# Linear attention with a feed-forward layer behind it: loads of v on other queues and in other memory, q transposed to contiguous columns, work of the first batches on other engines, and a new written order

## The chip, the cores and the metric

The kernel runs on one core of a Trainium2 chip. A core has five engines with instruction queues of their own: TensorE (PE, matmuls; its weight loads are shown as PEld), VectorE (DVE), ScalarE (ACT), GpSimd (POOL) and SyncE (SP). Each runs its instructions in the order in which they are written and waits on semaphores for the others. DMAs are issued from SP's queue and from GpSimd's, and are carried by 16 DMA engines. The metric is device time in microseconds (us). The kernel before takes 392.82 us, the median of 3 runs (391.64 to 393.09).

## The reference

Eight batches, eight heads, 576 tokens of 64 values. Each row of q and k is projected to 128 features, the largest absolute feature of the row is subtracted, and both signs go through the exponential. Then linear attention, and on its output, 4608 tokens of 512 values, a gated layer of width 1536:

```python
def phi(x):
    proj = np.einsum('bhsd,df->bhsf', x, w_phi)
    proj = proj - np.max(np.abs(proj), axis=-1, keepdims=True)
    return np.concatenate([np.exp(proj), np.exp(-proj)], axis=-1)
q_p, k_p = (phi(q), phi(k))
kv = np.einsum('bhsf,bhsd->bhfd', k_p, v)
z = np.sum(k_p, axis=2)
num = np.einsum('bhsf,bhfd->bhsd', q_p, kv)
den = np.einsum('bhsf,bhf->bhs', q_p, z)[..., None] + 1e-06
...
gate = np.maximum(x @ w_gate, 0.0)
val = x @ w_val
out = gate * val @ w_out
```

## The kernel before, in words

Each batch has 512 tokens, handled as four chunks of 128, and a remainder of 64; the remainders of two batches form a pair (four pairs, which make a ninth group for the feed-forward layer). The kernel is a list of small steps, named `do_xx` in the code. One long string, ORDER, names every step with its arguments (batch, group of heads, chunk, sign) and, after a colon, the PSUM banks that it uses. A loop walks the string and issues each step, so ORDER fixes by hand the order of each engine's queue, of SP's and of GpSimd's DMA issues too. Heads go in three groups, 0 to 1, 2 to 4 and 5 to 7.

The steps that matter here:

- Loads. `lk`, `lq`, `lm`, `ln` fetch k, q and their remainders on GpSimd's queue, converting to bf16. `lv` fetches v in fp32 on SP's queue into the one tile `vn`, and `lw` its remainder into `vm`. For batch 0, v lies without the column of ones. `wl` and `wo` fetch the weights of the feed-forward layer on GpSimd's queue, in thirds; `wp` and `wq` fetch the projection's weights on SP's, and `wc` and `wd` convert them on VectorE. `gt` is a tiny DMA that holds SP's queue until a group of k has landed. `ms` are memsets.
- k. For batch 0, `k0`, `k1`, `k2` transpose k on PE, copy it (VectorE) and project it. For later batches `kt` and `ku` transpose k in 32x32 blocks on VectorE, scattering the columns, and `kr` projects it on PE. `kx` takes the largest absolute value on VectorE, `ke` the exponentials of both signs on ScalarE, `kk` the factors exp(-m) and exp(m) into `ek`.
- v. `vs` and `vr` multiply v by these factors on GpSimd; `vo` writes the factors as the column behind v, which gives the denominator. `kv` multiplies k's features and v on PE, `kd` copies the result to the tile `kv` on VectorE.
- q. `qt` transposes q in 32x32 blocks on VectorE into `qT` (L607 to L614). `qc` (or `qs`, one quarter of it) projects it on PE: `q_cols` (L616) issues two sets of four matmuls, 32 rows and 512 columns each. `qe` takes the exponentials, `qx` the maxima by column, `qy`, `qz`, `qu`, `qw` turn the maxima into a factor a token.
- Output of attention. `nu` multiplies q's features with `kv` on PE; `nt`, `nv`, `nr` combine the two signs and take the reciprocal on VectorE. Then `ny` normalizes on VectorE or `nx` on GpSimd, into `xu`. For batch 0, `xp` transposes `xu` on PE and `xc` copies it into the tile of x^T; later `xt` does both as a DMA transposition on SP's queue. The four tiles of x^T are used in turn, batch by batch.
- Remainders: `mt`, `mc`, `me`, `mx`, `my`, `mz`, `mu`, `mw`, `mn`.
- Feed-forward: `fv` and `fg` (a group of 128 of the 1536 columns, four matmuls of 512 tokens each), `va` copies the value part on ScalarE, `ga` takes relu and product on VectorE; `fo` multiplies by the output weights in three parts, `oc` copies, `od` stores. For batch 0, two thirds of the columns are done by token chunk as `pv`, `pg`, `pa`, `pb`, so that they can begin when the first chunk of x^T is there. `zz` are dummy matmuls.

Of the kernel before, what the change touches and what calls it, by code (L numbers as in the profile page):

```python
# [8 lines left out]
FP32 = mybir.dt.float32  # L9
BF16 = mybir.dt.bfloat16  # L10
# [6 lines left out]
ms.0 wp ms.5 wq lk.0.0 ms.4 lk.0.1 lm.0.1 ms.3 lm.0.0 lk.0.2 wc id zz.10:0 k0.1:0 gt.0 lv.0.0 ms.2  # L17
lw.0.0 wd k1.1:0 lq.0.0 k0.0:1 k1.0:1 wl.0.1 zz.1:2 k2.1:2345 ke.0.1.3.1:5 ke.0.1.2.1:4 if
kx.0.1.0:2 k2.0:6701 kx.0.0.2:0 kx.0.0.1:7 kx.0.0.3:1 ke.0.1.3.0:5 lw.0.1 lq.0.1 ke.0.0.0.0:6
ke.0.0.0.1:6 ke.0.1.1.1:3 kx.0.0.0:6 kx.0.1.2:4 kx.0.1.3:5 k0.2:6 kk.0.0.0 ke.0.1.0.0:2  # L20
ke.0.1.0.1:2 kk.0.0.1 ke.0.0.2.1:0 kx.0.1.1:3 k1.2:6 wl.1.1 wl.0.0 lv.0.1 ke.0.0.1.1:7 wl.1.0
lm.1.1 ke.0.0.1.0:7 ke.0.1.1.0:3 qt.0.0.0 ke.0.0.3.1:1 qt.0.1.0 k2.2:5267 ke.0.1.2.0:4 kx.0.2.1:2
vr.0.0.0 kk.0.1.0 ke.0.0.2.0:0 qs.0.0.1:3 qx.0.0.1:3 vr.0.1.0 kk.0.1.1 ke.0.2.0.0:5 vs.0.0.1
ke.0.2.2.1:6 qs.0.0.0:4 ke.0.2.1.1:2 qx.0.0.0:4 qs.0.1.0:0 ke.0.2.1.0:2 kx.0.2.3:7 ke.0.0.3.0:1
qe.0.0.0.0:4 qx.0.1.0:0 kx.0.2.0:5 ke.0.2.3.0:7 kx.0.2.2:6 qy.0.0:2 qz.0.0:2 qe.0.1.0.0:0 vr.0.0.1
kk.0.2.0 vr.0.1.1 vs.0.0.0 qt.0.0.1 qs.0.1.1:1 ke.0.2.0.1:5 vo.0 ke.0.2.2.0:6 qx.0.1.1:1 kv.0.0:2
kd.0.0:2 qe.0.0.1.1:3 qt.0.1.1 qs.0.0.2:5 qx.0.0.2:5 vo.1 kk.0.2.1 qe.0.1.0.1:0 ke.0.2.3.1:7
qe.0.0.0.1:4 vs.0.1.0 vs.0.1.1 kv.0.1:6 kd.0.1:6 qs.0.1.3:2 qx.0.1.3:2 qe.0.0.1.0:3 lv.0.2
vs.0.2.0 vs.0.2.1 vo.2 qs.0.1.2:0 qe.0.1.2.1:0 qu.0.0 qw.0.0 nu.0.0.0:7 qe.0.1.3.1:2 qy.0.1:4
qz.0.1:4 ms.1 qu.0.1 qw.0.1 nt.0.0.0:7 nu.0.0.1:6 kv.0.2:3 nt.0.0.1:6 nv.0.0.0:7 qe.0.1.1.1:1  # L30
kd.0.2:3 qs.0.0.3:4 zz.1:7 nu.0.0.2:7 ln.0.0 lq.1.2 qx.0.0.3:4 zz.1:3 qy.0.3:3 nt.0.0.2:7
nv.0.0.1:6 qe.0.1.1.0:1 nu.0.1.1:1 qe.0.1.3.0:2 qe.0.0.2.0:5 nv.0.0.2:7 nr.0.0 lk.1.3 nu.0.1.0:2
nt.0.1.0:2 ny.0.0 nu.0.1.2:6 qe.0.1.2.0:0 qx.0.1.2:0 qz.0.3:3 zz.6:7 xp.0.0:7 xc.0.0:7 lm.1.0
nt.0.1.2:6 qe.0.0.3.1:4 nv.0.1.0:2 qy.0.2:0 qz.0.2:0 qe.0.0.3.0:4 nt.0.1.1:1 qe.0.0.2.1:5 qu.0.2
qw.0.2 nu.0.2.1:4 nu.0.2.0:5 nu.0.2.2:3 wl.1.2 nv.0.1.2:6 pv.0.0:7 pa.0.0:7 nv.0.1.1:1 ln.0.1
qu.0.3 nt.0.2.0:5 nr.0.1 nt.0.2.1:4 qw.0.3 wl.0.2 nu.0.3.2:2 nu.0.3.0:0 ny.0.1 nv.0.2.1:4
nt.0.2.2:3 nt.0.3.0:0 pg.1.0:6 nv.0.2.2:3 pv.1.0:1 xp.0.1:7 xc.0.1:7 nv.0.2.0:5 nv.0.3.0:0
pg.0.0:4 nr.0.2 ny.0.2 nt.0.3.2:2 pb.0.0:4 nv.0.3.2:2 qt.1.0 nu.0.3.1:3 nt.0.3.1:3 pv.1.1:7
pv.0.1:5 xp.0.2:0 pa.0.1:5 pa.1.0:1 xc.0.2:0 nv.0.3.1:3 pg.0.1:4 pb.0.1:4 pa.1.1:7 pg.1.1:2
qc.1.0:5103 qe.1.0.2.0:0 qe.1.0.3.0:3 qe.1.0.0.1:5 qe.1.0.2.1:0 pv.0.2:4 pa.0.2:4 nr.0.3 ny.0.3  # L40
# [36 lines left out]
qx.2.1.0:7 ln.1.1 fv.1.4:1 kv.2.1:0 qx.2.1.2:2 kk.2.2.1 lw.3.0 kv.2.0:3 kt.3.1 qy.2.0:5 qz.2.0:5
qe.2.1.3.0:4 kd.2.0:3 kk.2.2.0 kt.3.2 nr.8.0 qe.2.1.0.1:7 kd.2.1:0 fv.1.9:6 qe.2.1.0.0:7 fg.1.5:2
qu.2.0 va.1.4:1 qw.2.0 ga.1.5:2 nu.2.0.0:5 va.1.9:6 vs.2.2.0 vs.2.2.1 ln.1.0 ku.3 qe.2.1.3.1:4
qt.3.1 fv.1.3:7 nu.2.1.0:3 nt.2.1.0:3 kt.3.0 fv.1.6:1 va.1.3:7 nu.2.1.1:0 lv.3.1 nt.2.0.0:5  # L80
nv.2.0.0:5 nt.2.1.1:0 nv.2.1.1:0 kv.2.2:2 kd.2.2:2 fg.1.6:6 lv.3.3 qt.3.0 kr.3.0:4750 va.1.6:1
ga.1.6:6 ke.3.0.0.0:4 ke.3.0.1.1:7 lq.4.2 ke.3.0.0.1:4 nu.2.0.2:1 fg.1.3:2 nv.2.1.0:3 nu.2.0.1:6
nt.2.0.2:1 nv.2.0.2:1 nx.8.0 kx.3.0.0:4 xt.8.0 ga.1.3:2 ke.3.0.2.1:5 kx.3.0.2:5 fv.1.7:3 od.0.2
od.0.3 fg.1.4:1 nu.2.2.0:4 ga.1.4:1 nt.2.0.1:6 va.1.7:3 nv.2.0.1:6 ke.3.0.3.0:0 fv.1.10:2
nu.2.2.2:3 ke.3.0.1.0:7 nt.2.2.2:3 fv.1.8:1 kx.3.0.1:7 va.1.10:2 nv.2.2.2:3 fg.1.7:6 ke.3.0.3.1:0
ke.3.0.2.0:5 va.1.8:1 lm.4.1 kr.3.1:2753 ke.3.1.0.0:2 ke.3.1.1.0:7 lk.4.3 kx.3.0.3:0 kk.3.0.1
vr.3.1.1 ke.3.1.1.1:7 nu.2.2.1:0 ke.3.1.2.1:5 vr.3.0.1 nu.2.1.2:1 nt.2.2.0:4 nv.2.2.0:4 ga.1.7:6
ke.3.1.3.1:3 nt.2.2.1:0 fo.1.1.0:4 lv.3.2 nv.2.2.1:0 ke.3.1.3.0:3 kx.3.1.0:2 fv.1.11:6
ke.3.1.2.0:5 fg.1.10:0 lm.4.0 va.1.11:6 nt.2.1.2:1 nv.2.1.2:1 fg.1.9:1 kx.3.1.3:3 nr.2.0
# [146 lines left out]
def kernel(  # L236
# [16 lines left out]
    P = 128  # L253
# [70 lines left out]
    def xT(g):  # L324
        return xT_mix if g == B else xT_of(g)
# [620 lines left out]
```

## Time and profile before

| | |
|---|---|
| median of 3 runs | 392.82 us (391.64 to 393.09) |
| the profiled execution | 392.23 us, its span 390.4 us |
| PE busy | 370.0 us (95%) |
| VectorE busy | 281.3 us (72%) |
| ScalarE busy | 234.0 us (60%) |
| GpSimd busy | 157.1 us (40%) |
| PE's share of the chain that ended last | 84% |
| VectorE's share of it | 7% |

The span is what the profiler saw of the program; the execution's time is 1.8 us longer. Busy is the time in which an engine had an instruction in work. For PE the ends of matmuls are modelled and matmuls overlap, so small gaps between them count as busy. The chain that ended last goes back from the last instruction, at each step to what released it or to the one before it on its engine. A line of a group reads: line of the code, engine, operation, output and input tiles, shapes, count, then busy us, mean ns of one, and idle time before it.

### The profile page before, as it was taken

What the parts mean: (1) busy time and instruction counts of PE and PEld (TensorE: products, weight loads), DVE (VectorE), ACT (ScalarE), POOL (GpSimd) and SP (SyncE); (2) the same over time, 40 slices, a digit from 0 to 9 for tenths busy, and PEclk for the clock granted to TensorE, in tenths of its full rate; (3) what the DMA queues carried; (4) which work ended last, traced back from release to release, by engine and by line L of the source; (5) the groups of instructions that cost most, each with busy time, mean ns of one, the idle gap of its engine ahead of it and who ended that gap; (6) DMA issues with size and microseconds to landing.
All of it is one profiled execution on the core that took longest, in us unless ns stands there. A gap on an engine that the chain in (4) does not pass through costs nothing.

```text
span 390.4 us, 9052 instructions
## 1 busy us (share of the span) xinstructions
PE 370.0 (95%) x3536; PEld 196.8 (50%) x3536; DVE 281.3 (72%) x661; ACT 234.0 (60%) x560; POOL 157.1 (40%) x173
## 2 busy tenths in 40 slices
PE   3579999979999999999999999999999999999995
PEld 2247964645554465445544655465446544444442
DVE  3978998999999768489996978699856833320330
ACT  1855489898488822498779445988694313422312
POOL 8396048278544912258156622561561130100000
PEclk9999999989999999999999999999999999999999
DMA  8989995559497590272951695113620022101104
GB/s 109 212 158 189 198 185 95 110 90 135 67 194 105 100 168 13 70 140 52 179 99 56 89 206 84 38 38 66 143 81 3 2 54 109 40 0 55 54 0 107
DMA packets 91135, 38.01 MB, mean 97 GB/s; under 512 B 64214, under 2 KB 86486, under 8 KB 91094
## 3 DMA queue, kind: packets, MB, share of 16 engines
q0 software_dynamic: 33600, 14.18, 29.0%
q1 hardware_dynamic: 57494, 23.28, 26.5%
q8 instruction: 27, 0.44, 0.5%
q14 instruction: 14, 0.11, 0.1%
HBM read 37.95 MB, written 9.44 MB: 121 GB/s over the span
## 4 chain that ended last, share of the span: by engine, by line
PE 84%; DVE 7%; ACT 3%; POOL 2%; DMA 2%; issue 1%; DVEq 0%; ACTq 0%; POOLq 0%
PE bank L831 43%; PE bank L886 23%; PE bank L583 5%; PE bank L683 4%; PE bank L620 2%; PE bank L468 2%; ACT kp L515 2%; DMA kn<-in_k_dram 2%; POOL vs L544 1%; DVE kT L452 1%; DVE qT L611 1%; PE bank L857 1%; DVE h L875 1%; DVE mk L523 1%; DVE t L704 1%
## 5 line engine op out<-in xcount | busy, mean ns | idle before, releaser
L849 DVE SCALAR_TENSOR_TENSOR h<-bank,val 128x512 bf16<-128x512 f32 x100 | 66.6, 680 | 52.1 <-PE bank L831 27.6
L886 PE MATMUL bank<-wo,h 128*128 128x512 bf16 x432 | 100.2, 379 | 0.0
L846 ACT CAST val<-bank 128x512 bf16<-128x512 f32 x100 | 58.3, 607 | 62.1 <-PE bank L831 42.4
L515 ACT ACTIVATE kp<-bank 128x384 bf16<-128x384 f32 x192 | 81.9, 524 | 20.0 <-PE bank L468 8.8
L831 PE MATMUL bank<-xT,wv 128*128 128x512 bf16 x352 | 87.2, 382 | 0.0
L831 PE MATMUL bank<-xT,wg 128*128 128x512 bf16 x352 | 86.7, 379 | 0.3 <-DVE mk L523 0.3
L726 POOL TENSOR_TENSOR xu<-u,r 128x512 bf16<-128x512 f32 x32 | 33.1, 1042 | 104.9 <-DVE r L722 99.0
L635 ACT ACTIVATE qp<-bank 128x512 bf16<-128x512 f32 x128 | 70.1, 626 | 8.3 <-PE bank L620 6.6
L544 POOL TENSOR_TENSOR vs<-vn,ek 128x780 bf16<-128x780 f32 (+3 forms) x48 | 64.0, 1344 | 17.8 <-ACT ek L532 14.7
L886 PEld LDWEIGHTS <-h 128*128 128x128 bf16 x432 | 40.5, 98 | 46.9 <-issue 1.8
L831 PEld LDWEIGHTS <-wv 128*128 128x128 bf16 x400 | 37.1, 98 | 42.6 <-issue 3.9
L831 PEld LDWEIGHTS <-wg 128*128 128x128 bf16 x400 | 37.2, 98 | 41.9 <-issue 1.5
L523 DVE TENSOR_REDUCE mk<-bank 128x3 f32<-128x384 f32 x96 | 49.7, 545 | 7.6 <-ACT ob L895 4.7
L643 DVE TRANSPOSE_TENSOR_REDUCE maxq<-bank 128x16 f32<-128x512 f32 x64 | 42.7, 693 | 6.1 <-PE bank L620 3.0
L895 ACT COPY ob<-bank 128x512 f32<-128x512 f32 x36 | 21.3, 599 | 41.0 <-PE bank L886 40.3
L714 DVE TENSOR_TENSOR u<-bank,t 128x195 f32<-128x195 f32 (+1 forms) x108 | 34.5, 334 | 3.1 <-DVE t L704 0.5
L704 DVE TENSOR_TENSOR t<-bank,cq 128x195 f32<-128x195 f32 (+1 forms) x96 | 30.1, 327 | 4.9 <-PE bank L683 4.3
L683 PEld LDWEIGHTS <-qp 128*128 128x128 bf16 x512 | 25.1, 102 | 13.5 <-issue 2.1
L562 POOL TENSOR_TENSOR vr<-vm,ek 64x260 bf16<-64x260 f32 x32 | 19.7, 617 | 27.9 <-issue 11.0
L683 PE MATMUL bank<-kv,qp 128*128 128x65 bf16 x512 | 27.7, 199 | 0.7 <-DVE u L714 0.4
L583 PEld LDWEIGHTS <-kp 128*128 128x128 bf16 x640 | 24.2, 102 | 5.9 <-issue 1.1
L583 PE MATMUL bank<-vs,kp 128*128 128x65 bf16 x512 | 24.6, 200 | 1.1 <-POOL vs L555 0.7
(75 smaller groups left out, 314.2 us busy)
## 6 DMA issues: line engine op xcount, KB each, us to landing
out_dram<-ob SPq DMA_DIRECT2D x32, 256.0 KB, 2.9
vn<-in_v_dram SPq DMA_DIRECT2D x29, 256.0 KB, 5.7
qn<-in_q_dram POOLq DMA_DIRECT2D x7, 512.0 KB, 8.5
kn<-in_k_dram POOLq DMA_DIRECT2D x7, 512.0 KB, 8.7
wv<-in_moe_w_val_dram POOLq DMA_DIRECT2D x3, 512.0 KB, 16.3
wg<-in_moe_w_gate_dram POOLq DMA_DIRECT2D x3, 512.0 KB, 15.0
wo<-in_moe_w_out_dram POOLq DMA_DIRECT2D x3, 512.0 KB, 19.4
vm<-in_v_dram SPq DMA_DIRECT2D x16, 64.0 KB, 4.6
```

The lines of the kernel that those rows point to most:

```text
L515: nc.scalar.activation(kp_of(3 * b + j)[:, i, s].rearrange("p n f -> p (n f)"), bank[bk[0]][:, 0 : 3 * F], AF.Exp, scale=(1.0, -1.0)[s],)
L523: nc.vector.tensor_reduce(mk_of(3 * b + j)[:, :, i], bank[bk[0]][:, 0 : 3 * F].rearrange("p (n f) -> p n f", f=F), axis=AX.X, op=ALU.max, ...
L544: nc.gpsimd.tensor_tensor(vs_of(3 * b + j)[:, s, 0:n].rearrange("p n i e -> p (n i) e")[:, :, 0:e], src[:, lo:hi].rearrange("p h i e -> p ...
L583: nc.tensor.matmul(out_ps[:, h - lo, s, :], lhsT=lhsT, rhs=rhs, start=(at == 0), stop=(at == 2 * n * (C + 1) - 1),)
L635: nc.scalar.activation(qp_of(4 * b + i)[:, s, 4 * hq : 4 * hq + 4].rearrange("p h m -> p (h m)"), bank[bk[0]], AF.Exp, scale=(1.0, -1.0)[s],)
L643: nc.vector.tensor_reduce(maxq[:, :, i, 4 * hq : 4 * hq + 4].rearrange("p t h -> p h t"), bank[bk[0]].rearrange("p (h t u) -> p h t u", h= ...
L683: nc.tensor.matmul(bank[bk[0]][:, E * n : E * (n + 1)], lhsT=qp_of(4 * b + i)[:, s, h, :], rhs=kv_of(b)[:, h, s, :],)
L714: nc.vector.tensor_tensor(u_of(serial(b, i))[:, lo:hi], parts(bk, n)[:, :, 0], t_of(3 * serial(b, i) + g)[:, 0:n], op=ALU.add,)
L831: nc.tensor.matmul(bank[bk[0]], lhsT=w[:, dc, P * f : P * f + P], rhs=xT(g)[:, dc, :], start=(dc == 0), stop=(dc == NDC - 1),)
L846: nc.scalar.copy(val_of(NFC * g + f), bank[bk[0]])
L849: nc.vector.scalar_tensor_tensor(h2_of(g, f), bank[bk[0]], 0.0, val_of(NFC * g + f), op0=ALU.max, op1=ALU.mult)
L886: nc.tensor.matmul(bank[bk[0]], lhsT=h2_of(g, f)[:, P * t : P * t + P], rhs=wo_sb[:, f, :], start=(f == 0), stop=(f == NFC - 1),)
```

## The change

- `lv` of batch 0 is issued on GpSimd's queue. Its place there is behind groups of k and a half of q.
- v of batch 1 lands in the room of x^T tiles 2 and 3, which are now slices of one tile `xT_all` (L327 of the new code). It lies without the column of ones, so batch 1 has `vo` steps too. Batch 1's v needs no wait for batch 0's.
- `lq` loads the halves of batch 0's q by heads, not by partitions, and `qt` writes contiguous columns in one piece. The order of the tokens that the scattered write gave is now made by PE: `q_cols` reads its moving columns in the order h, t, c, with 128 bytes between neighbours.
- Batch 0, third group of heads: `kp` takes the factors into PSUM, and `vd` and `vp` do on VectorE what `vs` and `vo` did on GpSimd.
- `kc` copies kv of batches 0 and 1 on ScalarE, in place of `kd` on VectorE. Three of batch 0's four chunks are normalized by `nx` on GpSimd, in place of `ny`; the last two go through `xt` on SP's queue, in place of `xp` and `xc`.
- ORDER is new throughout. At its beginning it now reads as shown; `lk.0.1` comes first, and `wc` and `wd` come ahead of the memsets `ms.5`, `ms.3`, `ms.6`, `ms.4`. `lk.1.3` and `lq.1.2` (k and q of batch 1) come before most of the weights.

```diff
-ms.0 wp ms.5 wq lk.0.0 ms.4 lk.0.1 lm.0.1 ms.3 lm.0.0 lk.0.2 wc id zz.10:0 k0.1:0 gt.0 lv.0.0 ms.2
-lw.0.0 wd k1.1:0 lq.0.0 k0.0:1 k1.0:1 wl.0.1 zz.1:2 k2.1:2345 ke.0.1.3.1:5 ke.0.1.2.1:4 if
+ms.0 wp wc wq lk.0.1 wd ms.5 ms.3 ms.6 lq.0.0 lk.0.2 id lk.0.0 lm.0.0 lm.0.1 lv.0.1 ms.4 if
+zz.10:0 k0.1:0 k1.1:0 zz.3:1 k2.1:1234 ms.2 qt.0.0 ke.0.1.0.0:1 lq.0.1 ke.0.1.3.1:4 lm.1.0
...
-    xT_of = ring("xT", 4, [P, NDC, SF], BF16)
+    xT_all = sb.tile([P, 4, NDC, SF], BF16, name="xTs", tag="xTs")
...
-        return xT_mix if g == B else xT_of(g)
+        return xT_mix if g == B else xT_all[:, g % 4]
+
+    def v_one():
+        flat = xT_all[:, 2:4].rearrange("p s a b -> p (s a b)").bitcast(FP32)
+        return flat.rearrange("p (h c d) -> p h c d", c=C, d=D)
+
+    def v_in(b):
+        return v_one() if b == 1 else vn_of(b)
...
     def do_lq(bk, b, hq):
-        r = slice(SM * hq, SM * (hq + 1)) if hq < 2 else slice(0, P)
+        lo, hi = (4 * hq, 4 * hq + 4) if hq < 2 else (0, H)
         nc.gpsimd.dma_start(
-            out=qn_of(b)[r],
-            in_=q[b, :, 0:SF, :].rearrange("h (p c) d -> p h c d", c=C)[r],
+            out=qn_of(b)[:, lo:hi],
+            in_=q[b, lo:hi, 0:SF, :].rearrange("h (p c) d -> p h c d", c=C),
         )
...
         if b == 0:
             lo, hi = HEADS[i]
-            nc.sync.dma_start(
+            nc.gpsimd.dma_start(
                 out=v_flat()[:, lo:hi],
...
             nc.sync.dma_start(
-                out=vn_of(b)[:, :, i, 0:D],
+                out=v_in(b)[:, :, i, 0:D],
...
+    def ek_ps(bk, s):
+        return bank[bk[0]][:, 3 * F + 12 * s : 3 * F + 12 * s + 12]
+
+    def do_kp(bk, b, j, s):
+        nc.scalar.activation(
+            ek_ps(bk, s),
+            mk_of(3 * b + j).rearrange("p n i -> p (n i)"),
+            AF.Exp,
+            scale=(-1.0, 1.0)[s],
+        )
+
+    def do_vd(bk, b, j, s):
+        lo, hi = HEADS[j]
+        nc.vector.tensor_tensor(
+            vs_of(3 * b + j)[:, s].rearrange("p n i e -> p (n i) e")[:, :, 0:D],
+            v_flat()[:, lo:hi].rearrange("p h i e -> p (h i) e"),
+            ek_ps(bk, s)[:, :, None].to_broadcast([P, 12, D]),
+            op=ALU.mult,
+        )
+
+    def do_vp(bk, j):
+        nc.vector.tensor_copy(
+            vs_of(j)[:, :, :, :, D].rearrange("p s n i -> p s (n i)"),
+            bank[bk[0]][:, 3 * F : 3 * F + 24].rearrange("p (s n) -> p s n", s=2),
+        )
...
-    def do_qt(bk, b, hq, half=2):
-        r = slice(SM * half, SM * (half + 1)) if half < 2 else slice(0, P)
-        dst = qT_of(2 * b + hq)[r].rearrange("p h m a -> p (h m a)").bitcast(FP32)
-        src = qn_of(b)[r, 4 * hq : 4 * hq + 4].rearrange("p h c d -> p (h c d)").bitcast(FP32)
+    def do_qt(bk, b, hq):
         nc.vector.transpose(
-            dst.rearrange("p (h t c) -> p h c t", h=4, c=C),
-            src.rearrange("p (h c d) -> p h c d", c=C, d=R),
+            qT_of(2 * b + hq).rearrange("p h m a -> p (h m a)").bitcast(FP32),
+            qn_of(b)[:, 4 * hq : 4 * hq + 4].rearrange("p h c d -> p (h c d)").bitcast(FP32),
         )
...
-    def q_cols(T, which, banks, n):
+    def q_cols(T, which, banks, n, c):
...
-                    bank[bn][:, 0:n],
+                    bank[bn][:, 0:n].rearrange("p (h t c) -> p h t c", t=R, c=c),
                     lhsT=w32[r, a, :],
-                    rhs=T[r, :, :, a].rearrange("p h m -> p (h m)"),
+                    rhs=T[r, :, :, a].rearrange("p h (c t) -> p h t c", t=R),
...
     def do_qc(bk, b, hq):
-        q_cols(qT_of(2 * b + hq), range(4), bk, 512)
+        q_cols(qT_of(2 * b + hq), range(4), bk, 512, C)
...
     def do_mc(bk, p):
-        q_cols(qt_of(p), range(4), bk, 256)
+        q_cols(qt_of(p), range(4), bk, 256, 1)
```

## The prediction

> **What bounds the kernel now.** First the page, then busy time by stretch (columns: PE, PEld, DVE, ACT, POOL, clock, DMA share, GB/s).
>
> ```profile
> span 390.4 us, 9052 instructions
> PE 370.0 (95%) x3536; PEld 196.8 (50%) x3536; DVE 281.3 (72%) x661; ACT 234.0 (60%) x560; POOL 157.1 (40%) x173
> ...
> 10.00:20.00 10.00, 5.59 (x50) 2.85 (x49) 9.65 (x19) 8.96 (x27) 3.56 (x6) 1.00 1.19 214
> 50.00:60.00 10.00, 9.74 (x135) 6.24 (x133) 9.95 (x20) 9.06 (x22) 4.88 (x6) 1.00 1.29 182
> 70.00:80.00 10.00, 9.56 (x166) 5.88 (x166) 10.00 (x35) 7.57 (x21) 2.04 (x2) 1.00 0.56 116
> 80.00:90.00 10.00, 7.47 (x90) 3.85 (x87) 9.97 (x28) 9.77 (x28) 7.39 (x8) 0.83 0.68 106
> 200.00:300.00 100.00, 100.00 (x976) 50.83 (x975) 80.19 (x185) 71.62 (x173) 46.76 (x47) 1.00 0.44 85
> ```
>
> There are three stages: a start in which PE waits, a middle up to 90 us in which VectorE is hardly ever free and PE loses time once more (80 to 90), and a long rest in which PE is full. The chain of waits gives PE's pace, its timeline the two forms of the q projection:
>
> ```profile
> 62.48 2.59 PE bank L886 x12
> 65.07 0.56 PE bank L620 x8
> 65.63 0.74 PE bank L583 x20
> ...
> 69.95 0.41 PE L620 MATMUL bank<-qt,w 32*128 32x256 bf16 x8
> 70.29 0.30 PE L583 MATMUL bank<-vs,kp 128*128 128x65 bf16 x4
> ```
>
> A 512-column matmul goes by in 0.216 us (2.59 / 12), eight q matmuls on 32 rows in 0.56. Every group of matmuls at such a pace (1232 of 512 columns, 256 of 128 at 0.056, 1152 of 65 at 0.032, 128 for q at 0.070, the rest 20 us) sums to 346 us of work. The last group starts at 384.6, so PE waited 38: from start times less work done before them, 25.5 by 40 us, 27.6 by 80, 33.6 by 90, 38.0 at the end. The tail from there is 5.9. So 346 + 38 + 6 = 390.
>
> What sets the 33.6 is a debt: VectorE's work that must be done before a given PE step, less PE's own work before it. I count it through the written order, each instruction at the pace at which the timeline shows it following another (a reduction 0.46, a transposition of q 0.93, a product 0.60). Before, the debt is 13.7 at `fg.0.8` and 18.4 at `fv.1.0`. VectorE's chain begins with the copy of kT at 9.19, with 2.5 of its work done; so 18.4 - 2.5 + 9.2 = 25.1, and PE's 32.7 at `fv.1.0` leave 7.6 in which VectorE idled; at `fg.0.8` the same sum leaves 5.8.
>
> **The change, part by part.** VectorE first. The rows, by shape:
>
> ```profile
> L611 DVE STREAM_TRANSPOSE qT<-qn 128x512 f32<-128x512 f32 x14 | 15.2, 1086 | 0.0
> L452 DVE STREAM_TRANSPOSE kT<-kn 128x384 f32<-128x384 f32 x14 | 11.8, 853 | 0.0
> L452 DVE STREAM_TRANSPOSE kT<-kn 128x256 f32<-128x256 f32 x7 | 4.3, 617 | 0.0
> L457 DVE STREAM_TRANSPOSE kT<-km 128x128 f32<-128x128 f32 x7 | 1.9, 278 | 0.0
> L764 DVE STREAM_TRANSPOSE qt<-qm 128x256 f32<-128x256 f32 x4 | 1.7, 426 | 0.0
> L353 DVE MEMSET vn<- 128x32 f32 x1 | 0.1, 85 | 0.0
> L354 DVE MEMSET vm<- 128x4 f32 x1 | 0.1, 62 | 0.0
> ```
>
> L764 writes contiguously: with the 32-column one at 0.200 it gives 1.01 ns a column, so a contiguous q takes 0.69 instead of 1.09. Batch 0: four half turns of 1.08 become two (-2.9); batch 1: -0.8; later batches -0.4 each turn, not on the path. Of batches 0 and 1 also leave: six copies of kv (-3.0, by 0.55 and 0.41), three normalizations (-2.1), two copies of x^T (-0.8). New are two products of vs for the third group of heads, 768 columns from PSUM (by L704, 0.35 for 195 columns and 0.28 for 130: 0.94 each) and a small copy: +2.1. Net -7.5 before batch 1's FFN.
>
> ScalarE gets the six copies: 0.5 for 390 columns (between 0.25 for 12 and 0.60 for 512), 2.9 in all. Its debt by the same count rises only to 7.9 (before: 7.3), below VectorE's. GpSimd gives up two vs (2.9) and gets three normalizations (3.1), three small copies (0.8) and three DMA issues at 0.75. It stays behind VectorE's chain, but `vs.0.1.1` now stands behind `lq.1.2`, which waits for `qt.0.1`: some 18 us in, when it would start anyway. Eight PE transpositions go: -0.45.
>
> Against it: the new order puts `wd` ahead of the four big memsets. `wd` waits for its weight load until 7.30 now; two memsets, 1.1 apart at 1.30 and 2.40, then follow it, and the first kT copy starts near 10.3 instead of 9.19, although k of group 1, now first in the queue, lands some 1.3 earlier (8.28 before). SP's gate load `gt.0` waits for k of group 0, landing near 9.9, and the small v loads behind it follow. v of batch 1 no longer waits for vs of batch 0 (issued at 27.9 now): SP sends its four loads from 12 us, beside the weights. k of batch 1 is issued near 16 behind one third of wv; batch 1's k took 13.0 to land when issued at 29.6, so by 29 `kt.1.1`, standing in front of batch 0's products on VectorE, has it just in time. x^T of two quarters goes through SP's queue (2.5 quiet, 6.1 beside loads) and has about 6 until `pv.0.2`. I take these four at nothing; without that cover the start gives nothing back, which is a rival.
>
> In the new order the debt never passes 14.0 (`qc.1.0`). With 3.1 done at 10.3, that is 21.2; with VectorE idle 5.8 to 7.6 as before, PE's wait is 27 to 29 at 90 us instead of 33.6: **-5.6**. Rows after 90 stay.
>
> Then q on PE. It now reads its moving columns with 128 bytes from one to the next (four of them, then back). The trace has no such matmul. The two q rows give (0.56 - 0.34) us / 512 = 0.43 ns a column at a 4-byte step, against 0.42 contiguous. Lower end: no cost; the memset with a step of 260 bytes takes 0.82 ns an element, as fast as a contiguous one, and speaks for that; nothing in the change could make it a gain. Upper end: the transpositions, free at 8 bytes (L457), take 1.83 ns a column at 16; if a column of PE took as long, a set of four would take (1.83 - 0.43) x 512 = 0.72 more. Between: VectorE's factor, 1.83 / 1.01, on PE's 0.43, is 0.18 a set. I take this: it is the nearest row, the same kind of access on the other engine, as a share of that engine's own pace. Two sets a `qc`, 12 `qc` in batches 2 to 7, where PE is full and nothing hides them: 24 x 0.18 = **+4.3** (ends 0 and 17.2). Batches 0 and 1 lie under VectorE.
>
> [...]
>
> Sum: -5.6 - 0.5 + 4.3 = -1.8. The profiled execution took 392.23 (0.6 under the median of 392.82, inside 391.64 to 393.09); so 390.5.
>
> **Rivals.**
> - *Free columns*: PE reads the wide step at its old pace. The memset row speaks for it. 392.2 - 6.1 = 386.2.
> - *A line a column* (the other side): each column waits 1.8 ns, so `qc` takes 2.0 instead of 0.56, on the full PE. For it: the sharp edge between 8 and 16 bytes on VectorE. It makes the change slower from 0.25 us a set on. 392.2 - 6.1 + 17.2 = 403.3.
> - *The start gives nothing back*: VectorE stands before `kt.1.1` for k of batch 1, and batch 0's products behind it, because the early v loads share the DMA engines (share above 1 in 10 to 20 already). k at 35 instead of 29 eats the 5.6: 396. It decides from 3 us of lateness. Against it: v of batch 0 no longer competes from another queue, and k of batch 1 moves ahead of all weight loads but one.
>
> **How the numbers follow.** Forecast 0.35 (386.5 to 393.5 by its ends of start gain and of factor), free columns 0.31, a line a column 0.20, lost start 0.14. 0.5% of the median, about what a measurement of this kernel can tell, is 2.0: faster is below 390.9, slower above 394.8. Faster: all but 0.02 of free columns and half of the forecast, 0.47. Slower: the line case, 0.13 of the lost start, a trace of the forecast: 0.35. The rest, 0.18. The range runs from 384.5 (free columns and a debt paid 2 better) to 402.5, which leaves out half of the line case and little below.
>
> **What would show it.** `qT` transpositions near 690 ns; the matmuls of q eight in 0.9 (forecast), 0.56 (free) or 2.0 (a line). The first kT copy near 10.3. PE's busy time in 80 to 90 near 10 and no clock dip. VectorE below 9.5 from 60 us on. Wrong would make me: a wait of VectorE for `kn` near 30, of PE for `wo` near 70 (issued late in the new order, 18 to 20 to land before), or q at another pace.

## The result, and the profile after

The kernel after takes 404.14 us, the median of 4 runs (403.43 to 405.13), against 392.45 of before beside it (391.64 to 393.09): a ratio of 1.0301, with a 95% interval of 1.027 to 1.0332. It is slower by 3%, 1.6 us above the range given. The rival *A line a column*, 1.8 ns for each column of q, had 403.3. The execution that was profiled took 404.28.

The page of the kernel after, its span and the busy time of each engine:

```profile
span 402.4 us, 9064 instructions
...
PE 385.8 (96%) x3546; PEld 193.2 (48%) x3546; DVE 273.3 (68%) x651; ACT 238.7 (59%) x566; POOL 159.7 (40%) x179
```

Busy time by stretch, columns as in the table of before:

```profile
10.00:20.00 10.00, 9.10 (x70) 4.50 (x71) 8.59 (x20) 8.60 (x26) 6.80 (x8) 1.00 1.26 236
20.00:30.00 10.00, 8.69 (x46) 2.64 (x44) 7.25 (x15) 5.46 (x13) 7.83 (x12) 0.54 1.32 194
50.00:60.00 10.00, 10.00 (x131) 5.99 (x129) 8.80 (x17) 8.77 (x21) 8.93 (x12) 1.00 1.15 168
70.00:80.00 10.00, 8.38 (x123) 4.44 (x115) 8.31 (x25) 6.47 (x17) 4.79 (x5) 1.00 1.53 143
80.00:90.00 10.00, 10.00 (x86) 3.88 (x75) 7.93 (x19) 7.43 (x20) 7.63 (x9) 1.00 0.26 75
200.00:300.00 100.00, 100.00 (x900) 46.98 (x899) 73.08 (x173) 67.02 (x163) 39.64 (x41) 1.00 0.47 84
```

The hole in 80 to 90 is gone, and VectorE is no longer at 9.95 and more there. The granted clock, which dipped to 0.83 there before, is full; it now falls to 0.54 between 20 and 30, where before had 1.00. What that costs was not tried. But in 200 to 300, where PE was full before and is full now, it gets 900 matmuls done where it got 976. Busy time does not show that; the count does. The groups by line and shape say which matmuls grew (behind the first bar: busy us, mean ns of one; behind the second: idle time before them):

```profile
L651 PE MATMUL bank<-qT,w 32*128 32x512 bf16 x128 | 36.5, 1033 | 0.2 <-ACT kp L522 0.2
L642 DVE STREAM_TRANSPOSE qT<-qn 128x512 f32<-128x512 f32 x16 | 11.0, 690 | 0.0
L559 DVE TENSOR_TENSOR vs<-vn,bank 128x768 bf16<-128x768 f32 x2 | 1.9, 946 | 0.0
L628 ACT CAST kv<-bank 128x390 bf16<-128x390 f32 x4 | 1.9, 484 | 4.1 <-PE bank L617 4.0
```

The new VectorE and ScalarE rows came as priced (0.69 for q, 0.94 for a product, 0.5 for a copy of kv). The q matmul on PE (the four of a set start within some 10 ns of each other, and their times overlap) has a mean of 1033 ns; in the runs below that read and write contiguous columns it has 398 to 411. PE's timeline has eight of them at a time, beside the eight of 256 columns of a remainder, whose reading did not change, and one wait for a weight:

```profile
73.31 2.75 PE L917 MATMUL bank<-wo,h 128*128 128x512 bf16 x12 [1.62 <-DMA wo<-in_moe_w_out_dram]
...
123.15 1.90 PE L651 MATMUL bank<-qT,w 32*128 32x512 bf16 x8
130.90 1.91 PE L651 MATMUL bank<-qT,w 32*128 32x512 bf16 x8
140.81 0.41 PE L651 MATMUL bank<-qt,w 32*128 32x256 bf16 x8
```

From the first matmul of a `qc` to the first of the next step it is 1.837 us (1.834 to 1.839 over all fourteen); before, it was 0.56. That is 1.277 more each, 17.9 for fourteen. Without them the span would be 402.4 - 17.9 = 384.5, or 5.9 under before. So two things stand side by side: a start that gives back what was forecast, and a q projection that takes three times that. The experiments take them one at a time.

### The profile page after: what moved, and what is told of

Read it like the earlier page. It is cut to its first block, busy times and chain, and to the rows that moved or that the text cites. A ratio compares the mean times of both kernels' runs of the same rounds, so it can differ in the third digit from the quotient of the medians.

```text
span 402.4 us, 9064 instructions
## 1 busy us (share of the span) xinstructions
PE 385.8 (96%) x3546; PEld 193.2 (48%) x3546; DVE 273.3 (68%) x651; ACT 238.7 (59%) x566; POOL 159.7 (40%) x179
## 3 DMA queue, kind: packets, MB, share of 16 engines
q1 hardware_dynamic: 57510, 22.49, 27.5%
## 4 chain that ended last, share of the span: by engine, by line
PE 83%; DMA 7%; DVE 3%; POOL 2%; ACT 2%; issue 1%; SPq 0%; ACTq 0%; DVEq 0%; POOLq 0%
PE bank L862 40%; PE bank L917 22%; PE bank L651 8%; PE bank L617 5%; DMA wo<-in_moe_w_out_dram 4%; PE bank L714 3%; DMA out_dram<-ob 2%; PE bank L888 2%; PE bank L475 2%; DMA w64f<-in_w_phi_dram 1%; ACT kp L522 1%; POOL vs L577 1%; DVE t L735 1%; POOL vr L596 1%; PE bank L849 0%
## 5 line engine op out<-in xcount | busy, mean ns | idle before, releaser
L522 ACT ACTIVATE kp<-bank 128x384 bf16<-128x384 f32 x192 | 82.8, 512 | 27.1 <-PE bank L475 16.2
L757 POOL TENSOR_TENSOR xu<-u,r 128x512 bf16<-128x512 f32 x35 | 36.3, 1041 | 135.6 <-DVE r L753 102.9
L862 PE MATMUL bank<-xTs,wg 128*128 128x512 bf16 x352 | 87.4, 379 | 0.2 <-issue 0.2
L862 PE MATMUL bank<-xTs,wv 128*128 128x512 bf16 x352 | 86.0, 379 | 0.0
L577 POOL TENSOR_TENSOR vs<-vn,ek 128x780 bf16<-128x780 f32 (+3 forms) x40 | 52.8, 1337 | 37.3 <-ACT ek L539 20.4
L735 DVE TENSOR_TENSOR t<-bank,cq 128x195 f32<-128x195 f32 (+1 forms) x96 | 30.6, 329 | 10.3 <-PE bank L714 9.5
L651 PE MATMUL bank<-qT,w 32*128 32x512 bf16 x128 | 36.5, 1033 | 0.2 <-ACT kp L522 0.2
```

The costliest lines, as they stand in the source:

```text
L522: nc.scalar.activation(kp_of(3 * b + j)[:, i, s].rearrange("p n f -> p (n f)"), bank[bk[0]][:, 0 : 3 * F], AF.Exp, scale=(1.0, -1.0)[s],)
L577: nc.gpsimd.tensor_tensor(vs_of(3 * b + j)[:, s, 0:n].rearrange("p n i e -> p (n i) e")[:, :, 0:e], src[:, lo:hi].rearrange("p h i e -> p ...
L651: nc.tensor.matmul(bank[bn][:, 0:n].rearrange("p (h t c) -> p h t c", t=R, c=c), lhsT=w32[r, a, :], rhs=T[r, :, :, a].rearrange("p h (c t) ...
L862: nc.tensor.matmul(bank[bk[0]], lhsT=w[:, dc, P * f : P * f + P], rhs=xT(g)[:, dc, :], start=(dc == 0), stop=(dc == NDC - 1),)
```

## Experiments: the price of q on PE

Every ratio is to runs of the kernel before on the same chip. There were three sets: with 392.74 us of before (median of 7), the runs with q turned the old way, the kernel before with only q changed, the price list, and the order put right at the store; with 392.25 (13), the step on PSUM's side, the kernel before with split stores, the kv copies, and the memsets; with 392.01 (9), the other four.

**The new kernel with q turned the old way.** VectorE scatters the columns again, PE reads them contiguously; all else is the kernel after.

```diff
     def do_qt(bk, b, hq):
+        dst = qT_of(2 * b + hq).rearrange("p h m a -> p (h m a)").bitcast(FP32)
+        src = qn_of(b)[:, 4 * hq : 4 * hq + 4].rearrange("p h c d -> p (h c d)").bitcast(FP32)
         nc.vector.transpose(
-            qT_of(2 * b + hq).rearrange("p h m a -> p (h m a)").bitcast(FP32),
-            qn_of(b)[:, 4 * hq : 4 * hq + 4].rearrange("p h c d -> p (h c d)").bitcast(FP32),
+            dst.rearrange("p (h t c) -> p h c t", h=4, c=C),
+            src.rearrange("p (h c d) -> p h c d", c=C, d=R),
         )
...
-                    bank[bn][:, 0:n].rearrange("p (h t c) -> p h t c", t=R, c=c),
+                    bank[bn][:, 0:n],
-                    rhs=T[r, :, :, a].rearrange("p h (c t) -> p h t c", t=R),
+                    rhs=T[r, :, :, a].rearrange("p h m -> p (h m)"),
```

> The changed kernel with q turned the old way again (VectorE scatters, PE reads its columns 4 bytes apart); the order and all else as changed. Theory (each moving column that opens a line of its own costs PE about 1.7 ns, and the 14 qc lie on PE's path): 14 x 1.28 us go, 404.1 - 17.9 = 386.2, of which VectorE takes back up to 2 in the first two batches: 386 to 388. Rival (the loss comes from new stalls in the new order, the late wo and the loads at the start): 394 or more.

Measured: 386.31 us (385.71 to 388.51), a ratio of 0.9847 (0.9804 to 0.989) to before. `qc` is back at 0.56, and the group of its q matmuls at 411 ns:

```profile
L653 PE MATMUL bank<-qT,w 32*128 32x512 bf16 x128 | 14.0, 411 | 2.8 <-DVE qT L644 2.2 <-ACT kp L522 0.6
```

This one part of the change turns a kernel 1.5% faster than before into one 3% slower.

**The kernel before with only q changed.** The mirror image: contiguous turning and the step of 128 bytes on PE, in the old order.

```diff
-            dst.rearrange("p (h t c) -> p h c t", h=4, c=C),
-            src.rearrange("p (h c d) -> p h c d", c=C, d=R),
+            qT_of(2 * b + hq)[r].rearrange("p h m a -> p (h m a)").bitcast(FP32),
+            qn_of(b)[r, 4 * hq : 4 * hq + 4].rearrange("p h c d -> p (h c d)").bitcast(FP32),
...
-                    bank[bn][:, 0:n],
+                    bank[bn][:, 0:n].rearrange("p (h t c) -> p h t c", t=R, c=c),
-                    rhs=T[r, :, :, a].rearrange("p h m -> p (h m)"),
+                    rhs=T[r, :, :, a].rearrange("p h (c t) -> p h t c", t=R),
```

> The kernel before with q turned contiguously and PE reading with the wide step, nothing else. Theory: 14 qc x 1.28 = +17.9, the quarters of batch 0 cost up to 3 more beside other work, VectorE gives back up to 3 in its full stretch before 90 us: 392.5 + 15 to 18 = 407 to 411. Rival (the price is hidden in an order that has slack for it): under 400.

Measured: 410.85 us (409.73 to 411.2), a ratio of 1.0457 (1.0421 to 1.0492); 18.1 above before, for 17.9 of `qc`. The group of its q matmuls:

```profile
L618 PE MATMUL bank<-qT,w 32*128 32x512 bf16 x128 | 39.9, 1033 | 0.0
```

The same 1033 ns in the other order: the price belongs to the access, not to what runs beside it.

**Which distance, or which number of columns to 16 bytes?** The q projection of each batch from 2 on reads its 512 columns in another order, all of the same length, so that one trace holds a price list.

```diff
     def do_qc(bk, b, hq):
-        q_cols(qT_of(2 * b + hq), range(4), bk, 512, C)
+        form = {2: 2, 3: 4, 4: 8, 5: -2, 6: -4, 7: 1}.get(b)
+        if form:
+            q_step(qT_of(2 * b + hq), range(4), bk, form)
+        else:
+            q_cols(qT_of(2 * b + hq), range(4), bk, 512, C)
...
+                if form == 1:
+                    nc.tensor.matmul(dst, rhs=src.rearrange("p h m -> p (h m)"), **kw)
+                elif form == 2:
+                    nc.tensor.matmul(wide(dst), rhs=src.rearrange("p h (u w) -> p h w u", w=2), **kw)
...
+                elif form == -2:
+                    nc.tensor.matmul(dst.rearrange("p (t k e) -> p t k e", k=16, e=2), rhs=src.rearrange("p h (c t e) -> p t (h c) e", c=C, e=2), **kw)
```

> The changed kernel, in which the q projections of batches 2 to 7 read the same tile in another order of columns each, so that tokens, and in batches 5 and 6 heads too, are mixed up from there on (the amount of work is the same). Time of one qc, from its start to the next matmul's, by theory (one line of 16 bytes takes 1.7 ns, shared by the columns that lie in it and follow each other): batch 2, step 8 bytes, two columns a line: 0.97 us; batch 3, 16 bytes: 1.84; batch 4, 32 bytes: 1.84; batch 5, pairs of neighbours and then a jump: 0.97; batch 6, fours and then a jump: 0.56; batch 7, 4 bytes: 0.56. Total 395.6. [...] Second rival (the distance counts, not the line): batch 3 below batch 4, and both below 1.84.

Measured: 394.72 us, one execution. Its groups of q matmuls, one line a form (L670: 128 bytes; L660: 32; L658: 16; L656: 8; L662: two neighbours, then far away; L664: four neighbours, then far away; L654: contiguous, that is 4 bytes):

```profile
L670 PE MATMUL bank<-qT,w 32*128 32x512 bf16 x32 | 13.6, 1033 | 0.2 <-ACT kp L522 0.2
L660 PE MATMUL bank<-qT,w 32*128 32x512 bf16 x16 | 4.0, 1081 | 0.0
L658 PE MATMUL bank<-qT,w 32*128 32x512 bf16 x16 | 3.9, 1063 | 0.0
L656 PE MATMUL bank<-qT,w 32*128 32x512 bf16 x16 | 2.1, 615 | 0.0
L662 PE MATMUL bank<-qT,w 32*128 32x512 bf16 x16 | 2.1, 596 | 0.0
L664 PE MATMUL bank<-qT,w 32*128 32x512 bf16 x16 | 1.2, 380 | 0.0
L654 PE MATMUL bank<-qT,w 32*128 32x512 bf16 x16 | 1.3, 387 | 0.0
```

A mean includes more than the time until the next matmul can begin, so the price is better read from the start of one set of four to the start of the next in this trace:

| order of reading | columns in one 16-byte piece, one after another | set of four, ns | ns a piece |
|---|---|---|---|
| 128 bytes | 1 | 850 | 1.66 |
| 32 bytes | 1 | 896 | 1.75 |
| 16 bytes | 1 | 880 | 1.72 |
| 8 bytes | 2 | 430 | 1.68 |
| two neighbours, then far | 2 | 417 | 1.63 |
| four neighbours, then far | 4 | 233 | 1.82 |
| contiguous | 4 | 237 | 1.85 |

The last column is the set divided by 512 columns times the columns to a piece. Distance matters little (the steps of 16, 32 and 128 bytes differ by 5%); what counts is how many columns in a row lie in the same 16 bytes. Such a piece takes 1.63 to 1.75 ns whether one column or two are taken from it, and 1.82 to 1.85 with four. Four columns at PE's own pace (0.216 us for 512, so 1.69 ns for four) fill about that time, and a set takes 233 to 237 ns; two do not (417 to 430), and one leaves PE at about a quarter of its pace (850 to 896).

**The step on PSUM's side instead.** PE reads contiguously and writes each result where its token belongs, every fourth column of four bytes.

```diff
-                    bank[bn][:, 0:n].rearrange("p (h t c) -> p h t c", t=R, c=c),
+                    bank[bn][:, 0:n].rearrange("p (h t c) -> p h c t", t=R, c=c),
-                    rhs=T[r, :, :, a].rearrange("p h (c t) -> p h t c", t=R),
+                    rhs=T[r, :, :, a].rearrange("p h (c t) -> p h c t", t=R),
```

> The kernel after with the rearrangement of q on PE put on the other side: PE reads its moving columns contiguously, and writes them into PSUM in the order of the tokens (every 4th column of four bytes: a step of 16 bytes there). Theory (the price of the step is in reading SBUF's lines of 16 bytes, for the moving columns alone): eight matmuls of q in 0.56, as in the old order, and the time near 386. Rival (a step costs on PSUM's side too): eight matmuls well above 0.56; at the same 1.7 ns a column, 1.84, and 404.

Measured: 394.49 us, one execution, and both numbers were missed: a `qc` takes 0.97, a set 402 to 403 ns. The group:

```profile
L651 PE MATMUL bank<-qT,w 32*128 32x512 bf16 x128 | 23.7, 656 | 0.8 <-ACT kp L522 0.8
```

So writing with a step has a price of its own, 0.79 ns a column where the contiguous set has 0.46 and the stepped reading 1.66: some 0.3 more, where reading adds 1.2.

**The order put right at the store.** PE reads and writes contiguously, the tokens stay in the order in which they lie, and each store of 128 rows becomes four of 32.

```diff
-                    bank[bn][:, 0:n].rearrange("p (h t c) -> p h t c", t=R, c=c),
+                    bank[bn][:, 0:n],
-                    rhs=T[r, :, :, a].rearrange("p h (c t) -> p h t c", t=R),
+                    rhs=T[r, :, :, a].rearrange("p h m -> p (h m)"),
...
-            dst = out[S * g + P * t : S * g + P * (t + 1), :]
-            nc.sync.dma_start(out=dst, in_=ob_of(4 * g + t))
+            dst = out[S * g + P * t : S * g + P * (t + 1), :].rearrange("(u c) d -> c u d", c=C)
+            for cc in range(C):
+                nc.sync.dma_start(out=dst[cc], in_=ob_of(4 * g + t)[R * cc : R * (cc + 1)])
```

> The changed kernel with q turned contiguously, PE reading the columns as they lie, and the tokens of a chunk left in that order to the end: each store of a 128-row block becomes four stores of 32 rows, each fourth row. Theory: PE's price goes and VectorE keeps its shorter turns: 404.1 - 17.9 = 386.2, 385 to 387. Rival (96 more stores on SP's queue hold up the transpositions behind them): 389 or more.

Measured: 385.26 us (384.31 to 385.89), a ratio of 0.9802 (0.9764 to 0.984). No cost of the order shows here: VectorE has the 0.69, PE the 0.56, and from the start of the last matmul to the end it is 5.3 us, as in the kernel after, which has a quarter of these stores. The same kernel once more, as the common ground of the last four runs:

> The kernel after with q read contiguously and stores split in four, once more, as the common ground of this set: 384.8 to 386.

Measured: 384.65 us (384.25 to 386.89), 0.9818 (0.9792 to 0.9844). Against the run with the old turning the shorter one brings 1 us, and their intervals overlap. I call this kernel R below.

## Experiments: the start

**The kernel before with contiguous q and split stores** (the q part of the change alone, without its price):

> Before, with q turned contiguously and read by PE as it lies (no step of 128 bytes); the rows come out in another order, and each store is split in four stores of 32 rows. So the kernel before gets the cheaper turning without its price on PE, in an order in which VectorE is the bound up to 90 us. Theory (the debt on VectorE sets PE's 33.6 us of waits up to 90): two groups of four half turns of batch 0 become two turns (-2.9 in all, about half of it before the step at which the debt is highest) and batch 1's turns get 0.4 shorter each; PE's waits at 90 fall by 2 to 4, and the time from 392.7 to 389 to 391. Rival (something other than VectorE's turns sets those waits, or the shorter turns are eaten by the next wait): no change, 392 to 393.5. q matmuls eight in 0.56 by both.

Measured: 390.81 us (389.95 to 392.29, 10 runs), 0.9969 (0.9955 to 0.9984). The edit left batch 0's four half turns as four (0.69 instead of 1.08 each), not two as the expectation has it, so VectorE is spared 3.2 us up to batch 2: four half turns and four turns, 0.4 each. The time falls by 1.4. PE's waits (counted as in the prediction, from start times less work; dummy matmuls are not work, and matmuls without a record are counted in) are 32.2 where before had 33.6, so they fell by 1.4 and not by 2 to 4. The stretches of this run:

```profile
60.00:70.00 10.00, 9.95 (x144) 5.72 (x134) 8.60 (x19) 9.22 (x24) 8.15 (x7) 1.00 0.21 47
70.00:80.00 10.00, 9.38 (x143) 5.50 (x142) 10.00 (x37) 8.43 (x24) 2.92 (x3) 1.00 0.73 130
80.00:90.00 10.00, 7.59 (x78) 3.75 (x78) 9.13 (x22) 9.76 (x28) 8.49 (x11) 0.83 0.77 111
```

VectorE is idle for 1.4 us between 60 and 70 as before, and full between 70 and 80 as before; behind it, from 80 to 90, PE loses 5 us where before lost 6. Part of what VectorE saved earlier seems to have turned into idle time of its own (20 to 30: 6.81 busy, before 7.53). In this order, less than half of what is taken off VectorE reaches PE.

**R with the kv copies back on VectorE** (the six of batches 0 and 1; `kc` becomes `kd` in ORDER):

```diff
-vo.0 kv.0.2:3 kv.0.1:6 kc.0.2:3 lv.1.1 qe.0.1.1.0:0 qx.0.0.2:7 qw.0.0 nu.0.0.2:2 qx.0.0.3:5
+vo.0 kv.0.2:3 kv.0.1:6 kd.0.2:3 lv.1.1 qe.0.1.1.0:0 qx.0.0.2:7 qw.0.0 nu.0.0.2:2 qx.0.0.3:5
...
```

> The kernel after with q read contiguously (as the run that splits the stores in four, 385.3), and with the six kv copies of batches 0 and 1 back on VectorE (one part of the change undone: +3.0 us of VectorE's work, about 2.2 of it before batch 1's q projections, and 2.9 less on ScalarE). Theory (VectorE's debt sets PE's waits up to 50 us, so work given back to it is paid in full there): up to 3.0 more, 387 to 388.5. Rival (in the new order VectorE has slack by then, its copies hide beside PE): unchanged, 385 to 386.

Measured: 386.94 us (385.44 to 387.79), 0.9866 (0.9837 to 0.9895). It is 1.7 above R's 385.26 by the medians, and 2.5 by the ratios, since before differed by 0.5 between the two sets; PE's waits at 90 are 29.2 against 27.5. So more than half of the 3.0 put back is paid, though the intervals of the two ratios just touch.

**The new order with VectorE's old work.** The old turning of q, the kv copies, and three normalizations (`nx` becomes `ny`), all back on VectorE:

```diff
-ke.1.1.1.0:1 xc.0.0:2 nu.0.2.2:3 ke.1.1.3.0:0 nt.0.2.1:6 pv.0.0:5 nx.0.1 nt.0.2.2:3 ke.1.1.2.1:4
+ke.1.1.1.0:1 xc.0.0:2 nu.0.2.2:3 ke.1.1.3.0:0 nt.0.2.1:6 pv.0.0:5 ny.0.1 nt.0.2.2:3 ke.1.1.2.1:4
...
```

> The new order with VectorE's old work: q turned the scattered way (as the run that gave 386.3), and the six kv copies and three normalizations of batches 0 and 1 back on VectorE. That is +6.7 us of VectorE's work up to batch 1's FFN against the kernel after with shorter turns (four turns 0.4 each, 3.0, 2.1), so VectorE has about as much to do there as in the kernel before; the order of the steps stays the new one, and so do the queue of the first v and the room of batch 1's v. Theory A (the amount of VectorE's work sets PE's waits up to 90): nearly all is paid back, 390 to 393. Theory B (the new order of the steps, which feeds PE evenly between 70 and 90, brings most of the gain, and the work moved only the 1 and the 1.7 that its parts gave alone): 387.5 to 389.5.

Measured: 394.82 us (394.69 to 396.34), 1.0073 (1.005 to 1.0097): above both theories, slower than before, and 10.2 above R on the same chip, for 6.7 of work. PE's waits stand at 25.9 at 50 us, close to R's 24.9, and at 33.8 at 60, where R has 26.3. Its timeline there:

```profile
48.16 1.43 DVE L759 TENSOR_TENSOR xu<-u,r 128x512 bf16<-128x512 f32 x1
49.62 1.54 SPq L776 DMA_TRANSPOSE xTs<-xu  x1
58.08 1.89 PE L890 MATMUL bank<-xTs,wv 128*128 128x128 bf16 x16 [5.28 <-DMA xTs<-xu]
```

and that of R, as taken the second time:

```profile
44.33 1.04 POOL L757 TENSOR_TENSOR xu<-u,r 128x512 bf16<-128x512 f32 x1
45.40 1.21 SPq L774 DMA_TRANSPOSE xTs<-xu  x1
51.16 1.07 PE L888 MATMUL bank<-xTs,wv 128*128 128x128 bf16 x16 [1.12 <-DMA xTs<-xu]
```

The fourth quarter of x^T is normalized 3.8 later, behind VectorE's queue. Its DMA goes out 4.2 later, now behind two weight loads of 512 KB (issued at 46.75 and 48.96; in R the first of them at 46.06, after it), and takes 8.4 us to land instead of 5.7. PE waits 5.3 for it where R waits 1.1, and the clock falls to 0.79 between 50 and 60. In this trace, then, the new order depends on the work having been moved: a step late by some 4 us pushes a transfer into traffic, and the kernel pays 10.2 us for 6.7 of work. How much of the 10.2 would come from the order without that transfer was not tried.

**R with batch 0's v on SP's queue again:**

```diff
-            nc.gpsimd.dma_start(
+            nc.sync.dma_start(
                 out=v_flat()[:, lo:hi],
```

> The kernel after with q read contiguously (stores split in four), and batch 0's v issued on SP's queue again, at the same places of the order (one part of the change undone). SP's gate load waits for k of group 0 (landing near 10), so the three v loads would go out some us later, behind it. Theory (v of batch 0 is needed on GpSimd only from about 18 us on, and is there by then from either queue): unchanged, 385 to 386. Rival (v of batch 0 comes late and holds vs, and with it the kv products, back): 387 or more.

Measured: 386.32 us (384.05 to 388.49), 0.9839 (0.9792 to 0.9886). By the medians it is 1.7 above R, between the two cases. Its interval holds that of R, so the run does not tell whether this part brings anything.

**R with the memsets ahead of `wc` and `wd`:**

```diff
-ms.0 wp wc wq lk.0.1 wd ms.5 ms.3 ms.6 lq.0.0 lk.0.2 id lk.0.0 lm.0.0 lm.0.1 lv.0.1 ms.4 if
+ms.0 ms.5 ms.3 ms.4 ms.6 wp wc wq lk.0.1 wd lq.0.0 lk.0.2 id lk.0.0 lm.0.0 lm.0.1 lv.0.1 if
```

> The kernel after with q read contiguously (385.3), and the four big memsets of VectorE moved ahead of its small copies wc and wd, where they were before. wd waits for its weight load until 7.3 us and holds the memsets and the first copy of kT (10.0) behind it. Theory (the start of VectorE's chain sets PE's waits): the first kT copy starts near 8 instead of 10.0, but k of group 2 lands only at 9.6 and of group 0 at 10.3, so of the 2 us 1 to 2 are kept: 383.3 to 384.5. Rival (the loads of k bound the start, not the memsets): 385 to 386.

Measured: 383.65 us (381.37 to 384.48), 0.9777 (0.9742 to 0.9812). Once more, beside R:

> The kernel after with q read contiguously and the four memsets ahead of wc and wd, once more, beside the next run on the same chip: 383.0 to 384.5, and 1 to 2.5 below the next run if the place of the memsets is worth what its single comparison said; within 0.7 of it if that was chance.

Measured: 383.77 us (381.9 to 384.54), 0.9773 (0.9745 to 0.98), against 384.65 of R: 0.9 below by the medians, between the two cases, and the intervals of the two ratios overlap. Taken together, the nine runs with the memsets ahead lie between 381.37 and 384.54 us, the nine of R between 384.25 and 386.89, and the ratios to before (0.9777 and 0.9773 against 0.9802 and 0.9818) say the same in both sets. So the place of the memsets is worth something, 1 to 2 us by these figures. This kernel is the fastest of the study, faster than before and than after. VectorE's start by the timeline, in the kernel after and then in this second run:

```profile
7.34 0.45 DVE L349 CAST w<-w64f 128x128 bf16<-128x128 f32 x1 [2.16 <-DMA w64f<-in_w_phi_dram]
7.62 0.17 DVE L364 MEMSET maxq<- 128x128 f32 x1
7.87 0.93 DVE L362 MEMSET vr<- 128x1040 bf16 x1
8.77 0.17 DVE L365 MEMSET maxm<- 128x128 f32 x1
9.10 0.93 DVE L363 MEMSET vr<- 128x1040 bf16 x1 [0.17 <-issue]
9.94 0.16 DVE L355 CAST identf<-ident 128x128 f32<-128x128 bf16 x1
10.02 0.55 DVE L500 COPY kT<-bank 128x768 bf16<-128x768 bf16 x1
```

```profile
7.67 0.23 DVE L349 CAST w<-w64f 128x128 bf16<-128x128 f32 x1 [1.94 <-DMA w64f<-in_w_phi_dram]
7.81 0.22 DVE L355 CAST identf<-ident 128x128 f32<-128x128 bf16 x1
7.95 0.55 DVE L500 COPY kT<-bank 128x768 bf16<-128x768 bf16 x1
```

In the changed order, 2.3 us of memsets sit between the late weight and the first copy of k, though they need nothing that is late. Where `wd` began at 8.71 (the second trace of R), that copy slid on to 11.39.

## Why the prediction was right or wrong, point by point

**The failed step: the price of q on PE.** "Between: VectorE's factor, 1.83 / 1.01, on PE's 0.43, is 0.18 a set. I take this: it is the nearest row". Measured: 0.61 a set (850 - 238 ns), 1.277 a `qc`. The upper end, 0.72 a set by 1.83 ns a column, was nearly it. The mistake was to carry over a ratio. What came out nearly the same on both engines is the time of a column that has 16 bytes for itself: 1.83 ns on VectorE, 1.66 on PE. The rows of before even fit a time per 16-byte piece: at 8 bytes, where two columns share a piece, VectorE takes 2 x 1.01 = 2.02, which covers 1.83. By this estimate an engine with 1.01 a column pays little; one with 0.43 pays the difference, 1.83 - 0.43.

That one limit stands behind both numbers is not shown. The transposition was not "the same kind of access": it reads contiguously and takes its step in writing, while PE takes it in reading. The memset with a step of 260 bytes, the row that spoke for free columns, writes with a step too and pays nothing (0.82 ns an element), and PE's own writing with a step, into PSUM, took 0.79 ns a column. So no row of before was a witness for an engine that reads with a step, and that the upper end came so near is in part luck. The price of the reading itself is measured by the runs.

**What was added to it.** Twelve `qc` at the measured price are 15.3 instead of 4.3: 11.0 of the miss. "Batches 0 and 1 lie under VectorE" was nearly right: at 70 us PE's waits are 28.7 in the kernel after and 27.1 in R, so 1.6 of the dearer q of these batches is paid. The wait for `wo` adds 1.2 against R. 390.5 + 11.0 + 1.6 + 1.2 = 404.3, and 404.14 was measured; that it closes so well is in part luck, since the 390.5 rests on a start that R beat. From R's profiled execution, 385.47, the same terms (15.3, 1.6 and 1.2) lead to 403.6, where the kernel after had 404.28: 0.7 stays open. The rival *A line a column* came nearest with 403.3, with the set too dear (0.72) and batches 0 and 1 left out.

**The start: -5.6, and -0.45 for the transpositions.** 392.2 - 6.1 = 386.2 was written for free columns. R is that kernel, with contiguous turns and no price on PE, and takes 385.26 and 384.65, 0.9 to 1.6 less; its waits of PE at 90 are 27.5, in the 27 to 29 forecast. The kernel after with the old turning takes 386.31, with waits of 28.2, but its VectorE has 1.6 us (four turns, 0.4 each) more to do than the sum counts, so that it meets 386.2 is chance. The size held, then. The count of VectorE's debt as a law is weaker than its result. In the old order 3.2 us of shorter turns brought 1.4; in the new one, 3.0 put back cost 1.7 to 2.5, and 6.7 put back cost 10. The part of the relief that was tried without the new order brought little, and the new order without most of the relief was slower than before: the gain needs both, and the runs don't split it between them.

**What was taken at nothing.** k of batch 1 was issued at 15.9 and landed at 23.6, and VectorE never waited for it: *The start gives nothing back* did not come about. The first copy of kT came at 10.02 (forecast 10.3), and the runs with the memsets moved, 383.65 and 383.77 beside R's 385.26 and 384.65, put 1 to 2 us on their place: this part was not free. x^T through SP's queue was not free: the last quarter landed in 4.6 us in the kernel after (6.1 beside loads was the figure used) and PE did not wait for it, but in R, where PE is earlier, it waits 1.8 in all for the two quarters.

**The sign named for `wo`.** PE did wait for it near 70: 1.62 us at 73.31. The last two thirds were issued at 57.65 and 58.46 in the kernel after, and the last took 14.8 us; in R they go out 2.3 earlier, and PE waits 0.4. So most of this wait seems a follow-up of the slow q, not a fault of the order.

**The other signs.** `qT` at 690 ns, PE at 10.00 in 80 to 90 without a dip of the clock, eight q matmuls at 1.84: the first two as forecast, the third nearest the 2.0 of the rival. VectorE stayed below 9.5 from 60 on except for 9.66 between 60 and 70.

## What to carry to other kernels

When an access pattern moves from one engine to another, do not carry over the slowdown as a ratio: a fast engine can lose much more than a slow one to the same time per column (here PE went from 0.46 to 1.66 ns, VectorE from 1.01 to 1.83). Measure the pattern on the new engine, in one `qc` of one trace if need be. Where PE reads, here, divide the time of a 16-byte piece (1.63 to 1.75 ns) by the columns that are taken from it one after another, and compare with PE's pace. Where PE is full, a rearrangement belongs on whoever has slack, here the stores, which did it without a cost that shows. A count of an engine's work says which engine matters, but what a relief is worth is decided by the places where that engine waits, and by the transfers that start behind it (here one that landed in 8.4 us instead of 5.7).

## What was not expected of the hardware

**Two columns to a 16-byte piece are not enough for PE.** An 8-byte step, free for VectorE's transpositions before (278 ns for 128 columns), takes PE 430 ns a set, and pairs take 417, where four neighbours take 233.

**The 128-byte step keeps its pace where contiguous reading takes longer.** A stretch of the kernel after (PE's busy time, granted clock, DMA share, GB/s):

```profile
25.00:30.00 5.00, 5.00 (x39) 0.50 1.33 193
```

and its q matmuls there, from the timeline:

```profile
26.44 1.90 PE L651 MATMUL bank<-qT,w 32*128 32x512 bf16 x4
```

The same stretch of R, and its timeline:

```profile
25.00:30.00 5.00, 5.00 (x80) 0.60 1.31 187
```

```profile
25.77 1.03 PE L651 MATMUL bank<-qT,w 32*128 32x512 bf16 x4
```

And the same of the kernel before, contiguous too:

```profile
25.00:30.00 5.00, 4.45 (x59) 1.00 0.55 90
```

```profile
26.55 1.04 PE L620 MATMUL bank<-qT,w 32*128 32x512 bf16 x4
```

The two pairs of the kernel after start 853 ns apart at a clock of 0.50, as its sets do later at full clock (850 to 855). In R, contiguous, they are 406 apart at 0.60, and 236 to 240 later, at full clock. But in the kernel before they are 408 apart here at a clock of 1.00. So the granted clock does not explain why contiguous pairs take longer in this stretch; what does is not shown, and neither is why the 128-byte read takes no longer there. The step on PSUM's side behaves otherwise. In that run's trace the clock is 0.52 between 20 and 30, and there its sets start 753 ns apart, against 402 to 403 later, at full clock:

```profile
27.93 1.89 PE L651 MATMUL bank<-qT,w 32*128 32x512 bf16 x4
```

**A step on PSUM's side has its own price**, 402 to 403 ns a set against 236 to 240, for 16 bytes from one column written to the next.
